# Wider conversion blocks (384 or 512 columns instead of 256) for the later weights of an attention and mixer kernel

## The chip, the cores and the metric

The kernel runs on one core of a Trainium2 chip. The metric is the device time of one execution in microseconds (us), from start to end. Before the change it was 773.08 us, the median of three runs (770.61, 773.08, 774.40).

## What is computed

The reference has three parts in a row, for 4 batches of 576 tokens with 512 features:

```python
# 1. attention, 8 heads of 64: a local band plus an average-pooled attention
out = repeat(softmax(qd kd^T) vd, 4) + softmax(band(q k^T)) v
# 2. mixer: a token mix and a channel mix, both with ReLU
u = x + (relu(x^T w_tok1) w_tok2)^T
x = u + relu(u w_ch1) w_ch2                # w_ch1 512x1536, w_ch2 1536x512
# 3. a second mixer
theta = x w_theta                          # 512x512
y = w_tok_r (x cos theta) + w_tok_i (x sin theta)
u = x + y
out = u + relu(u w_ch)                     # 512x512
```

The attention inputs are float32. The weights arrive as 64-bit floats, since they were divided by a square root on the host. The kernel reads them as pairs of 32-bit words and turns each into two float32 parts, a high and a low one, whose sum carries more digits than one of them. All large products are made from such parts: a matmul of high with high, one of high with low, one of low with high.

## The kernel before

**Order of the work.** The attention, the token mix and the first half of the channel mix for batches 0 and 1 are interleaved by a list written out by hand (`ORDER`). After it come the loops of line 644 (first half of the hidden channels, batches 2 and 3), of line 677 (second half, batches 0 to 3) and of line 780 (the second mixer). TensorE is never told to wait for a stage as a whole: the framework's scheduler lays out one instruction order for each engine from the program's order, from the dependencies and from an estimate of each instruction's length, and on the chip each engine takes its list in order.

**The channel mix** (`channel_mix`, line 187) works on one batch and, by `th`, on one half of its tokens (288) at a time. It loads `ut` through the SyncE queue (L198), splits it into `uh` and `ul` (L97 on ScalarE, L98 on VectorE), and makes six blocks of hidden channels, each of 12 matmuls (L101 to L103). Each block leaves PSUM by two instructions, a ReLU on ScalarE (L217) and a subtraction on VectorE (L218), both at high priority. These give `g`, the high and low part of the hidden values. Then come four blocks of outputs, each of 18 matmuls (L226, L227 with the high `g` of all six hidden blocks, then L229 with the low `g`), and each is added to `ut` by VectorE (L231). One such half of a batch has 144 matmuls, 72 of each product.

**The conversion** (`weights`, line 109) takes one block of a weight: a DMA into a staging buffer `raw` (L114, here through ScalarE's queue, `rawq[0] = nc.scalar`), then

- ScalarE: L122 (low word to `wf`) and L124 (absolute value of the high word to `ww`),
- GpSimd: L125, a clamp of `ww`,
- VectorE: L129, L137 and L140 on the bits of `ww`, L147 on `wf`,
- ScalarE: L148, the high part; GpSimd: L149, a subtraction; and L150, an addition that gives the low part, in turn on GpSimd and on VectorE.

The staging buffers `ww`, `we` and `wf` have 3 slots each, and `raw` has 4. `load_split` (line 155) makes a list of such steps for one weight, column block by column block and in each over the row blocks of 128.

**What is converted beside the channel mix.** The second half of `w_ch1` (tiles `c11h`, `c11l`: 12 blocks of 256 columns), the second half of `w_ch2` (`c21h`, `c21l`: 12 blocks), `w_theta` (`thh`, `thl`: 8 blocks), the joined `w_tok_r` and `w_tok_i` (`wrh`, `wrl`: 18 blocks of 288) and `w_ch` (`wch`, `wcl`: 8 blocks), 58 blocks in this order. `channel_mix` takes them from `aside`, 6 at the end of each half of a batch: in four halves by line 645, in six by line 678. `c11` and `c21` are needed by the loop of line 677, the others by that of line 780.

Of the kernel before, what the change touches and what calls it, by code (L numbers as in the profile page):

```python
# [36 lines left out]
B, H, S, D = 4, 8, 576, 64  # L37
DM = H * D
# [23 lines left out]
def kernel(  # L62
# [19 lines left out]
    nc = tc.nc  # L82
# [5 lines left out]
    xT_d = [dram.tile([DM, S], F32, name=f"xT_{b}") for b in range(B)]  # L88
# [15 lines left out]


    clamps = chain(islice(cycle([pool] * 4 + [dve]), 33), repeat(pool))
    rawq = [nc.sync]

    def weights(stage, hi, lo, parts, adder=dve):

        n = hi.shape[-1]
        raw = stage.tile([128, n], parts[0][2].dtype, tag="raw", name="raw", bufs=4)
        for p0, p1, src in parts:
            rawq[0].dma_start(raw[p0:p1], src)  # L114
        if raw.dtype == I64:
            words = raw.bitcast(U32).rearrange("p (n t) -> p n t", t=2)
            high = raw.bitcast(F32).rearrange("p (n t) -> p n t", t=2)[:, :, 1]
            w = stage.tile([128, n], F32, tag="ww", name="ww")
            e = stage.tile([128, n], BF16, tag="we", name="we")
            f = stage.tile([128, n], BF16, tag="wf", name="wf")  # L120

            act.activation(f, words[:, :, 0], AF.Copy, scale=2.0**-52)  # L122

            act.activation(w, high, AF.Abs)  # L124
            next(clamps).tensor_scalar(  # L125
                out=w, in0=w, scalar1=F64_LEAST, scalar2=F64_MOST, op0=ALU.max, op1=ALU.min
            )
            wu = w.bitcast(U32)
            dve.tensor_scalar(  # L129
                out=wu,  # L130
                in0=wu,
                scalar1=3,
                scalar2=0x3FFFFFF8,
                op0=ALU.logical_shift_left,
                op1=ALU.bitwise_and,
            )
            dve.scalar_tensor_tensor(  # L137
                out=wu, in0=words[:, :, 1], scalar=0xC0000000, in1=wu, op0=ALU.bitwise_and, op1=ALU.bitwise_or
            )
            dve.tensor_scalar(  # L140
                out=e.bitcast(U16),
                in0=w.bitcast(U16).rearrange("p (n t) -> p n t", t=2)[:, :, 1],
                scalar1=0xFF80,
                scalar2=None,
                op0=ALU.bitwise_and,
            )
            dve.tensor_tensor(out=f, in0=f, in1=e, op=ALU.mult)  # L147
            act.copy(hi, w)  # L148
            pool.tensor_tensor(out=w, in0=w, in1=hi.bitcast(F32), op=ALU.subtract)  # L149
            adder.tensor_tensor(out=lo, in0=w, in1=f, op=ALU.add)  # L150
        else:
            adder.tensor_copy(hi, raw)
            pool.tensor_tensor(out=lo, in0=raw, in1=hi.bitcast(F32), op=ALU.subtract)

    def load_split(pool_, stage, name, src, nk, n, chunk, adders=(pool, dve)):

        hi = pool_.tile([128, nk, n], F32R, name=name + "h")
        lo = pool_.tile([128, nk, n], F32R, name=name + "l")
        steps = []
        for c in range(0, n, chunk):  # L160
            for k in range(nk):
                def step(k=k, c=slice(c, c + chunk), adder=adders[len(steps) % len(adders)]):
                    weights(stage, hi[:, k, c], lo[:, k, c], [(0, 128, src[k * 128 : (k + 1) * 128, c])], adder)
                steps.append(step)
        return hi, lo, steps
# [7 lines left out]
    NCH = DCH // 2  # L173
    NCB = NCH // 128

    def channel_weights(pool_, stage, half):
        c = slice(half * NCH, (half + 1) * NCH)
        adders = (pool, dve) if half else (pool,)
        h1, l1, s1 = load_split(pool_, stage, f"c1{half}", w_ch1[:, c], 4, NCH, 256, adders)
        h2, l2, s2 = load_split(pool_, stage, f"c2{half}", w_ch2[c, :], NCB, DM, 256, adders)  # L180
        return (h1, l1, h2, l2), s1 + s2


# [3 lines left out]
    def channel_mix(b, half, src, dst, w, mmb, queue, aside=(), per=0):  # L187

        w1h, w1l, w2h, w2l = w
        for th in range(2):  # L190
            t = slice(th * HALF, (th + 1) * HALF)
            at = f"{b}_{half}_{th}"
            here = half == 0 and b in DIRECT
            if here:
                ut = mixed[b][th]
            else:
                ut = b2.tile([128, 4, HALF], F32, tag="ut", name=f"ut_{at}")
                queue.dma_start(ut, uT_d[b][:, t].rearrange("(k p) n -> p k n", p=128))  # L198
            uh = b1.tile([128, 4, HALF], F32R, tag="uh", name=f"uh_{at}")
            ul = b1.tile([128, 4, HALF], F32R, tag="ul", name=f"ul_{at}")  # L200
            if here:
                for kb in range(4):
                    split(uh[:, kb, :], ul[:, kb, :], ut[:, kb, :])
            else:
                split(uh, ul, ut)
            if half:
                queue.dma_start(ut, src[:, t].rearrange("(k p) n -> p k n", p=128))
            hs = []
            for cb in range(NCB):
                c = slice(cb * 128, (cb + 1) * 128)  # L210
                ps = mmb.tile([128, 512], F32, tag="mb", name=f"c1_{at}_{cb}")
                for kb in range(4):
                    mm3(ps[:, 0:HALF], w1h[:, kb, c], w1l[:, kb, c], uh[:, kb, :], ul[:, kb, :], kb == 0, kb == 3)
                h1 = hp.tile([128, HALF], F32R, tag="h1", name=f"g1_{at}_{cb}")
                h2 = hp.tile([128, HALF], F32R, tag="h2", name=f"g2_{at}_{cb}")
                with tc.high_priority(offset=2000):
                    act.activation(h1, ps[:, 0:HALF], AF.Relu)  # L217
                    dve.scalar_tensor_tensor(  # L218
                        out=h2, in0=ps[:, 0:HALF], scalar=0.0, in1=h1.bitcast(F32), op0=ALU.max, op1=ALU.subtract
                    )  # L220
                hs.append((h1, h2))
            for db in range(4):
                d = slice(db * 128, (db + 1) * 128)
                ps = mmb.tile([128, 512], F32, tag="mb", name=f"c2_{at}_{db}")
                for cb in range(NCB):
                    pe.matmul(ps[:, 0:HALF], w2h[:, cb, d], hs[cb][0], start=(cb == 0), stop=False)  # L226
                    pe.matmul(ps[:, 0:HALF], w2l[:, cb, d], hs[cb][0], start=False, stop=False)  # L227
                for cb in range(NCB):
                    pe.matmul(ps[:, 0:HALF], w2h[:, cb, d], hs[cb][1], start=False, stop=(cb == NCB - 1))  # L229
                with tc.high_priority(offset=2000):  # L230
                    dve.tensor_tensor(out=ut[:, db, :], in0=ps[:, 0:HALF], in1=ut[:, db, :], op=ALU.add)  # L231
            queue.dma_start(dst[:, t].rearrange("(k p) n -> p k n", p=128), ut)
            for st in islice(aside, per):
                st()

    with ExitStack() as actx:
        sb1 = actx.enter_context(tc.tile_pool(name="a1", bufs=1))
        sb2 = actx.enter_context(tc.tile_pool(name="a2", bufs=2))
        stg = actx.enter_context(tc.tile_pool(name="stg", bufs=3))
# [53 lines left out]
        low, lowsteps = channel_weights(wlow, stg, 0)  # L293
# [329 lines left out]
        for e in ORDER:  # L623
            if e == "S":
                spare.release()
                spare = None
                mmb = tc.alloc_tile_pool(name="mmb", bufs=2, space=PSUM, side="right")
# [7 lines left out]
            else:  # L635
                event(e[0], int(e[1:]))

    rawq[0] = nc.scalar
    mmw = tc.alloc_tile_pool(name="mmw", bufs=6, space=PSUM)
    wide = tc.alloc_tile_pool(name="whigh", bufs=1)  # L640
    stg = tc.alloc_tile_pool(name="stg", bufs=3)
    high, highsteps = channel_weights(wide, stg, 1)
    aside = iter(highsteps)
    for b in range(sum(e[0] == "C" for e in ORDER), B):
        channel_mix(b, 0, None, xT_d[b], low, mmb if b == B - 2 else mmw, nc.sync, aside, 6)
    wlow.release()
    cw = ctx.enter_context(tc.tile_pool(name="cw", bufs=1, side="right"))
    thh, thl, thsteps = load_split(cw, stg, "th", w_theta, 4, DM, 256)
    wch, wcl, wcsteps = load_split(cw, stg, "wc", w_ch, 4, DM, 256)
    wrh, wrl, wrsteps = load_split(cw, stg, "wr", w_ri, 9, S, HALF)  # L650
    aside = iter(thsteps + wrsteps + wcsteps)
    cx = ctx.enter_context(tc.tile_pool(name="cx", bufs=2, side="right"))
# [22 lines left out]
        return xh, xl  # L675

    for b in range(B):
        channel_mix(b, 1, xT_d[b], xT_d[b], high, mmw, nc.sync, aside, 6)
        if b == B - 2:
            xx = stage_x(0, mmw)  # L680
            stg.release()
            cs = ctx.enter_context(tc.tile_pool(name="cs", bufs=1, side="right"))
            xhl = split_x(0, xx[0])
# [183 lines left out]
```

## Time and profile before

| what | value |
|---|---|
| median of three runs | 773.08 us |
| profiled execution | 770.8 us, of which its span on the engines is 768.9 us |
| TensorE matmul | 714.6 us busy (93%), 7872 matmuls |
| VectorE | 509.6 us (66%) |
| ScalarE | 333.6 us (43%) |
| GpSimd | 265.4 us (35%) |
| mean granted TensorE clock | 0.973 of full speed |

A busy TensorE is not TensorE at its peak, since matmuls overlap. The shares are means over stages that differ: the conversions of the last 58 blocks lie between about 314 and 480 us of the span, and what they cost is read there.

### The profile page before, as it was taken

The page shows a single profiled execution, that of the slowest core. Times are in us where ns is not written, and L with a number is a line of the kernel's source. Part 1 is how long each engine was busy: PE and PEld are TensorE (multiplying, and loading weights), DVE is VectorE, ACT ScalarE, POOL GpSimd, SP SyncE. Part 2 cuts the span into 40 slices and gives each one's busy share as a digit, 9 for nine tenths or more (in the row PEclk, how much of TensorE's full clock was granted, in tenths as well). Part 3 has the DMA queues.
Part 4 walks back from the last instruction along what each step waited for, and adds up shares of the span by engine and source line. Part 5 has one row for each costly group of instructions (what it writes and reads, how often), then busy time and mean ns, then how long its engine had stood idle before and what let it go on. Part 6 is the DMA issues. An engine that isn't in the chain of part 4 may idle for free.

```text
span 768.9 us, 19289 instructions
## 1 busy us (share of the span) xinstructions
PE 714.6 (93%) x7872; PEld 672.6 (87%) x7872; DVE 509.6 (66%) x1151; ACT 333.6 (43%) x774; POOL 265.4 (35%) x292
## 2 busy tenths in 40 slices
PE   8586978789999999899999899999999999999998
PEld 5365766679979999899999889999999999999998
DVE  5998999985565334499999999422585365554432
ACT  1564656534244222356555555231574254353310
POOL 1767687671021000398998887000000000000000
PEclk9777999899999999999999999999999999999999
DMA  9578656654343220545565856330000400300101
GB/s 274 179 200 220 185 147 196 180 167 141 129 134 102 66 78 32 165 153 170 171 186 172 256 166 192 116 93 32 32 1 1 131 1 1 124 1 1 64 1 62
DMA packets 61897, 90.73 MB, mean 118 GB/s; under 512 B 10096, under 2 KB 39920, under 8 KB 61808
## 3 DMA queue, kind: packets, MB, share of 16 engines
q1 hardware_dynamic: 53456, 73.70, 31.5%
q10 hardware_dynamic: 8352, 15.80, 6.7%
q8 instruction: 62, 1.02, 0.6%
q14 instruction: 27, 0.22, 0.1%
HBM read 69.42 MB, written 20.05 MB: 116 GB/s over the span
## 4 chain that ended last, share of the span: by engine, by line
PE 60%; DVE 23%; DMA 6%; issue 6%; POOL 2%; SPq 2%; ACT 1%; ACTq 0%; DVEq 0%; POOLq 0%
PE y L103 5%; PE y L101 5%; PE y L102 5%; PE c L229 4%; PE c L226 4%; PE c L227 4%; DVE ww L137 4%; DVE ww L129 3%; PE c L101 3%; PE c L103 3%; PE c L102 3%; DVE wf L147 3%; DVE we L140 3%; PE th L101 2%; PE th L102 2%
## 5 line engine op out<-in xcount | busy, mean ns | idle before, releaser
L125 POOL TENSOR_SCALAR ww<-ww 128x256 f32<-128x256 f32 (+1 forms) x85 | 100.3, 1182 | 55.6 <-ACT ww L124 51.2
L103 PE MATMUL y<-wrh,zl 128*128 128x288 f32 x256 | 75.7, 296 | 0.0
L102 PE MATMUL y<-wrl,zh 128*128 128x288 f32 x256 | 75.6, 295 | 0.0
L101 PE MATMUL y<-wrh,zh 128*128 128x288 f32 x256 | 75.6, 296 | 0.0
L218 DVE SCALAR_TENSOR_TENSOR g<-c,g 128x288 fp32r<-128x288 f32 x96 | 43.2, 451 | 44.0 <-ACT g L217 43.9
L217 ACT ACTIVATE g<-c 128x288 fp32r<-128x288 f32 x96 | 38.9, 408 | 57.0 <-PE c L103 55.2
L101 PE MATMUL c<-uh,c10h 128*128 128x288 f32 x192 | 58.6, 310 | 3.7 <-DVE g L218 3.7
L122 ACT ACTIVATE wf<-raw 128x256 bf16<-128x256 uint32 (+1 forms) x91 | 40.4, 444 | 45.5 <-DVE wrl L150 8.3
L226 PE MATMUL c<-g,c21h 128*128 128x288 f32 x192 | 54.6, 306 | 5.7 <-ACT g L217 5.7
L102 PE MATMUL c<-ul,c10h 128*128 128x288 f32 x192 | 57.2, 299 | 1.0 <-DVE ul L98 1.0
L103 PE MATMUL c<-uh,c10l 128*128 128x288 f32 x192 | 57.5, 300 | 0.0
L101 PE MATMUL c<-uh,c11h 128*128 128x288 f32 x192 | 56.9, 296 | 0.0
L102 PE MATMUL c<-ul,c11h 128*128 128x288 f32 x192 | 56.6, 295 | 0.0
L103 PE MATMUL c<-uh,c11l 128*128 128x288 f32 x192 | 56.5, 294 | 0.0
L129 DVE TENSOR_SCALAR ww<-ww 128x256 uint32<-128x256 uint32 (+1 forms) x91 | 50.0, 551 | 6.3 <-POOL ww L125 5.8
L227 PE MATMUL c<-g,c21l 128*128 128x288 f32 x192 | 53.7, 301 | 0.0
L226 PE MATMUL c<-g,c20h 128*128 128x288 f32 x192 | 53.0, 302 | 0.7 <-ACT g L217 0.5
L227 PE MATMUL c<-g,c20l 128*128 128x288 f32 x192 | 53.3, 300 | 0.0
L137 DVE SCALAR_TENSOR_TENSOR ww<-raw,ww 128x256 uint32<-128x256 uint32 (+1 forms) x91 | 49.1, 541 | 1.5
L102 PEld LDWEIGHTS y<-wrl,zh 128*128 128x128 f32 x256 | 48.1, 188 | 0.0
L101 PEld LDWEIGHTS y<-wrh,zh 128*128 128x128 f32 x256 | 48.1, 188 | 0.0
L103 PEld LDWEIGHTS y<-wrh,zl 128*128 128x128 f32 x256 | 48.1, 188 | 0.0
(201 smaller groups left out, 2243.5 us busy)
## 6 DMA issues: line engine op xcount, KB each, us to landing
raw<-w_ch ACTq DMA_DIRECT2D x32, 256.0 KB, 2.8
ut<-uT SPq DMA_DIRECT2D x14, 576.0 KB, 4.5
xT<-ut SPq DMA_DIRECT2D x14, 576.0 KB, 3.2
raw<-w_ch SPq DMA_DIRECT2D x24, 256.0 KB, 3.5
vd<-vtok SPq DMA_DIRECT2D x8, 650.0 KB, 7.2
raw<-w_ri ACTq DMA_DIRECT2D x18, 288.0 KB, 3.1
k<-kT SPq DMA_DIRECT2D x16, 291.0 KB, 5.7
q<-qT SPq DMA_DIRECT2D x16, 288.0 KB, 4.8
```

What stands on the lines that cost most here:

```text
L101: pe.matmul(out, lh, rh, start=start, stop=False)
L102: pe.matmul(out, lh, rl, start=False, stop=False)
L103: pe.matmul(out, ll, rh, start=False, stop=stop)
L122: act.activation(f, words[:, :, 0], AF.Copy, scale=2.0**-52)
L125: next(clamps).tensor_scalar(out=w, in0=w, scalar1=F64_LEAST, scalar2=F64_MOST, op0=ALU.max, op1=ALU.min)
L129: dve.tensor_scalar(out=wu, in0=wu, scalar1=3, scalar2=0x3FFFFFF8, op0=ALU.logical_shift_left, op1=ALU.bitwise_and,)
L137: dve.scalar_tensor_tensor(out=wu, in0=words[:, :, 1], scalar=0xC0000000, in1=wu, op0=ALU.bitwise_and, op1=ALU.bitwise_or)
L217: act.activation(h1, ps[:, 0:HALF], AF.Relu)
L218: dve.scalar_tensor_tensor(out=h2, in0=ps[:, 0:HALF], scalar=0.0, in1=h1.bitcast(F32), op0=ALU.max, op1=ALU.subtract)
L226: pe.matmul(ps[:, 0:HALF], w2h[:, cb, d], hs[cb][0], start=(cb == 0), stop=False)
L227: pe.matmul(ps[:, 0:HALF], w2l[:, cb, d], hs[cb][0], start=False, stop=False)
L229: pe.matmul(ps[:, 0:HALF], w2h[:, cb, d], hs[cb][1], start=False, stop=(cb == NCB - 1))
```

## The change

The later weights are converted in wider blocks: `c11` in blocks of 384 columns, `c21`, `th` and `wc` in blocks of 512. The joined token weights `wr` keep 288. The `raw` staging buffer has 3 slots instead of 4 in these stages, and `channel_mix` takes 4 steps (line 645) or 5 (line 678) at the end of a half instead of 6. In blocks: `c11` 12 to 8, `c21` 12 to 6, `th` 8 to 4, `wc` 8 to 4, `wr` 18 as before, so 58 become 40.

```diff
-    rawq = [nc.sync]
+    rawq, rawn = [nc.sync], [4]
...
-        raw = stage.tile([128, n], parts[0][2].dtype, tag="raw", name="raw", bufs=4)
+        raw = stage.tile([128, n], parts[0][2].dtype, tag="raw", name="raw", bufs=rawn[0])
...
-        h1, l1, s1 = load_split(pool_, stage, f"c1{half}", w_ch1[:, c], 4, NCH, 256, adders)
-        h2, l2, s2 = load_split(pool_, stage, f"c2{half}", w_ch2[c, :], NCB, DM, 256, adders)
+        n1, n2 = (NCH // 2, DM) if half else (256, 256)
+        h1, l1, s1 = load_split(pool_, stage, f"c1{half}", w_ch1[:, c], 4, NCH, n1, adders)
+        h2, l2, s2 = load_split(pool_, stage, f"c2{half}", w_ch2[c, :], NCB, DM, n2, adders)
...
-    rawq[0] = nc.scalar
+    rawq[0], rawn[0] = nc.scalar, 3
...
-        channel_mix(b, 0, None, xT_d[b], low, mmb if b == B - 2 else mmw, nc.sync, aside, 6)
+        channel_mix(b, 0, None, xT_d[b], low, mmb if b == B - 2 else mmw, nc.sync, aside, 4)
...
-    thh, thl, thsteps = load_split(cw, stg, "th", w_theta, 4, DM, 256)
-    wch, wcl, wcsteps = load_split(cw, stg, "wc", w_ch, 4, DM, 256)
+    thh, thl, thsteps = load_split(cw, stg, "th", w_theta, 4, DM, DM)
+    wch, wcl, wcsteps = load_split(cw, stg, "wc", w_ch, 4, DM, DM)
...
-        channel_mix(b, 1, xT_d[b], xT_d[b], high, mmw, nc.sync, aside, 6)
+        channel_mix(b, 1, xT_d[b], xT_d[b], high, mmw, nc.sync, aside, 5)
```

## Rows read from the trace of the kernel before

**Rows 1.** Stretches: length, then busy PE, PEld, DVE, ACT, POOL (instructions), clock, DMA, GB/s.

```profile
373.00:405.00 32.00, 31.07 (x230) 30.41 (x229) 30.61 (x74) 19.14 (x48) 29.26 (x32) 1.00 0.65 198
405.00:460.00 55.00, 50.19 (x354) 48.45 (x353) 52.49 (x110) 30.53 (x73) 46.29 (x46) 0.97 0.63 195
460.00:481.47 21.47, 20.55 (x151) 19.84 (x150) 20.28 (x48) 11.87 (x29) 16.06 (x18) 1.00 0.66 207
481.47:500.65 19.18, 19.18 (x146) 19.18 (x145) 8.46 (x16) 4.75 (x9) 0.00 (x0) 1.00 0.32 99
```

**Rows 2.** Timeline of PE (start, length, what): the starts of products.

```profile
362.70 0.29 PE L226 MATMUL c<-g,c20h 128*128 128x288 f32 x1
...
374.05 0.30 PE L101 MATMUL c<-uh,c11h 128*128 128x288 f32 x1
...
383.65 0.30 PE L226 MATMUL c<-g,c21h 128*128 128x288 f32 x1
...
481.47 0.29 PE L101 MATMUL c<-uh,c11h 128*128 128x288 f32 x1
...
491.07 0.30 PE L226 MATMUL c<-g,c21h 128*128 128x288 f32 x1
...
500.65 0.60 PE L665 MATMUL ct<-idt,cx 128*128 128x128 f32 x4
```

**Rows 3.** Who waited for whom, 310 to 485 us: total us, times, longest us.

```profile
ACT c21h L148 <- DVE ww L137: 6.8, 9, 2.0
PE c L226 <- ACT g L217: 6.2, 10, 1.6
```

**Rows 4.** Timelines of POOL, DVE and ACT around 361 us and around 428 us.

```profile
360.32 1.24 POOL L125 TENSOR_SCALAR ww<-ww 128x256 f32<-128x256 f32 x1 [0.29 <-ACT ww L124]
361.25 0.29 DVE L147 TENSOR_TENSOR wf<-wf,we 128x256 bf16<-128x256 bf16 x1
...
426.94 0.87 POOL L149 TENSOR_TENSOR ww<-ww,wrh 128x288 f32<-128x288 f32 x1
427.06 0.92 DVE L129 TENSOR_SCALAR ww<-ww 128x288 uint32<-128x288 uint32 x1
...
428.75 0.43 ACT L148 CAST wrh<-ww 128x288 fp32r<-128x288 f32 x1 [0.93 <-DVE ww L137]
429.14 0.41 ACT L217 ACTIVATE g<-c 128x288 fp32r<-128x288 f32 x1
```

**Rows 5.** Two stretches of 2 us, in the columns of rows 1.

```profile
430.00:432.00 2.00, 2.00 (x10) 2.00 (x9) 1.97 (x6) 2.00 (x5) 1.71 (x3) 0.50 1.05 391
432.00:434.00 2.00, 2.00 (x12) 2.00 (x12) 1.97 (x4) 1.03 (x3) 1.69 (x3) 0.69 0.93 303
```

**Rows 6.** Groups by shape, 310 to 485 us: busy us, mean ns, idle before.

```profile
L150 DVE TENSOR_TENSOR thl<-ww,wf 128x256 fp32r<-128x256 f32 x4 | 1.7, 413 | 0.0
L150 DVE TENSOR_TENSOR wrl<-ww,wf 128x288 fp32r<-128x288 f32 x9 | 4.0, 445 | 0.0
```

**Rows 7.** Timeline of DVE: two additions and what follows the first.

```profile
384.48 0.41 DVE L150 TENSOR_TENSOR c21l<-ww,wf 128x256 fp32r<-128x256 f32 x1
384.81 0.28 DVE L147 TENSOR_TENSOR wf<-wf,we 128x256 bf16<-128x256 bf16 x1
...
479.56 0.43 DVE L150 TENSOR_TENSOR wcl<-ww,wf 128x256 fp32r<-128x256 f32 x1 [0.26 <-POOL ww L149]
```

**Rows 8.** Timelines of ACT and PE where the conversions begin.

```profile
314.18 1.38 ACTq L114 DMA_DIRECT2D raw<-w_ch  x3
320.51 0.43 ACT L122 ACTIVATE wf<-raw 128x256 bf16<-128x256 uint32 x1 [1.53 <-DMA raw<-w_ch]
...
322.10 0.40 PE L101 MATMUL c<-uh,c10h 128*128 128x288 f32 x1 [1.66 <-DVE g L218]
```

**Rows 9.** DMA issues, 310 to 485 us: count, KB each, median us to landing.

```profile
raw<-w_ch ACTq DMA_DIRECT2D x32, 256.0 KB, 2.8
raw<-w_ri ACTq DMA_DIRECT2D x18, 288.0 KB, 3.1
```

## Prediction

> **What bounds the kernel now.** I read the table of stretches first. While the conversions run, TensorE is busy nearly all the time, but VectorE is as full: 30.61 of 32 us, 52.49 of 55, 20.28 of 21.47 [rows 1]. In the stretch after them TensorE has no gap and VectorE is under half busy. Next I read the starts of the products in TensorE's timeline, because a modelled busy time hides small gaps. Undisturbed, one half of a batch takes 500.65 - 481.47 = 19.18 us, its second product 500.65 - 491.07 = 9.58 [rows 2]. The five halves before took 481.47 - 374.05 = 107.4 us [rows 2], so 11.5 us more than 5 x 19.18, some 2.3 each. The loss sits in the second product: that of 362.70 lasted to 374.05, 11.35 us in place of 9.58, so 1.77 lost [rows 2]. The list of waits says why: L226 stood ten times for the ReLU L217, 6.2 us, and ScalarE's L148 nine times for VectorE's L137 in one weight alone, 6.8 us [rows 3]. The timelines join the two. GpSimd's subtraction L149 ran from 426.94 to 427.81; VectorE's L129, begun at 427.06, ended just after it, 0.92 us long; L137 followed, L148 on ScalarE waited for it, and the ReLU behind L148 began only at 429.14 [rows 4], with TensorE waiting. In this gap the granted clock fell to 0.50 for 430 to 432 us, the lower of its two levels, 1.2 GHz [rows 5], after TensorE had stood; 10 and 12 matmuls in 2 us each there, where the pace of rows 2 gives 15. So the ceiling of any gain is the loss of this stage, some 15 us (11.5 + 1.8, and 1.7 at the start, below); from 481 us on TensorE alone sets the time.
>
> **The change part by part.** *Fewer, longer instructions.* 40 blocks of 256 become 22 wider ones: 18 are gone, the columns stay. On VectorE L150 takes 413 ns for 256 columns and 445 for 288 [rows 6]: 1.0 ns a column, so 413 - 256 = 157 ns of a block are not owed to its columns. A block has four more VectorE instructions, and every second block an L150; I give each the same 157 ns as an estimate: 4.5 x 0.157 = 0.71 us for a block gone. That is the upper end. The lower one: L147 starts 0.33 us after an L150 of 0.41 us [rows 7], so 0.08 of the 157 ns lies beside the next instruction: 4.5 x 0.077 = 0.35 us. Between them 0.53, so VectorE is rid of 18 x 0.53 = 9.5 us (6.3 to 12.8). It is the fullest engine, so the last block, which ended at 479.99 [rows 7], would end at about 470.5. ScalarE saves too, but it has 30.53 of 55 us busy [rows 1]: nothing, beside other work. If its cover goes, it is again the wait for L137 that shows, priced below.
>
> *What this does for TensorE.* The last disturbed half (460.62 to 481.47; its length is near the mean of the five) lost 1.7 us, and in its second product, from 470.2 on. With the conversions over by then this goes: **-1.7 us** (0 to -1.7). For the second products from 362.70 and 383.65, with `c21` and `th` beside them, two things can happen. If as many columns per half are converted as now (8 blocks a half, so 4 mergers), VectorE has 4 x 0.53 = 2.1 us less to do in a half that loses 1.77, and the loss goes: -3.4 for both. If the columns come faster instead, VectorE is as full as before and the loss stays: 0. And if each wait is as long as its instruction, it doubles: +3.4. Nothing in the order holds the columns back, as VectorE at 30.61 of 32 shows, so I take a value near the middle one: **-0.8 us**.
>
> *The waits on the shared memory path.* A VectorE instruction of the conversion that starts beside GpSimd's two-input L149 ends after it, while one beside the clamp L125 does not wait for its end: L147 took 0.29 us at 361.25, inside a clamp that ran until 361.56 [rows 4]. Half as many waits of twice the length change VectorE's sum by nothing, which is what I take; their length is priced in the second rival. The Trainium skill, "SBUF — State Buffer", section "SBUF: two separate sides", states that VectorE and GpSimd share a port pair under an exclusive lock, and that whichever starts first holds it for its whole instruction while the other fully blocks. The trace agrees for L149 and not for the clamp. By that rule the wider clamp would stop VectorE for all of its length, and my sum would come to no gain (third rival).
>
> *The start.* Three loads are issued from 314.18 on; ScalarE stood 1.53 us for the third until 320.51, and TensorE then 1.66 us [rows 8]. The first blocks are 384 KB instead of 256. 288 KB landed in 3.1 us and 256 in 2.8 [rows 9]: 0.3 us for 32 KB, so +1.2 for 128. The far end: all 320.51 - 314.18 = 6.33 us scale by 1.5, +3.2; the near end 0, if the ReLU stands ahead of that wait in ScalarE's list. The scheduler can place it so; I take **+0.5 us**.
>
> *Slots and steps.* With 3 `raw` slots two loads run ahead of the block in work. Blocks come every 163 / 58 = 2.8 us now, some 4 after, so a load has 8 us for the 3 to 5 it takes: nothing; if this cover is gone, ScalarE waits for a load as in [rows 8], 1.5 us each. Steps of 4 and 5 for 6 only set the place in the program, and blocks don't keep to it: the last of `c21`, put behind the half that ends at 374.05, ran until 384.89 [rows 2, 7], and the last of `wc`, put behind the one that ends at 500.65, by 479.99. Nothing. The loads issued from ScalarE's queue fall by 18; ScalarE has room. The `wr` blocks are the same; their losses, with the clock's fall, may move either way by what the fall cost, 5 + 3 matmuls of 0.13 us [rows 5], 1.1 us.
>
> *Sum.* -1.7 - 0.8 + 0.5 = -2.0 us. The profiled execution was 770.8 us (span 768.9 and 1.9 around it), so 768.8 against it. The median of the runs, 773.08, stands 2.3 above that execution: 771.1 us.
>
> **The rivals.**
> 1. *VectorE drops below TensorE's pace.* The 2.1 us less per half are more than the loss of 1.77, so the small difference decides. -1.7 - 3.4 = -5.1, with the clock's fall gone -6.2: 768.0 to 766.9. For it: the loss is a thin excess of VectorE's work. Against it: the full VectorE of rows 1, which takes all that is offered. Chance 0.33.
> 2. *Longer waits, slower.* A ReLU behind an L148 waits for an L137 that waits for a GpSimd instruction of 512 columns. Place: the second products from 362.70 and 383.65 and that beside `wc`. If each loss doubles: 1.77 + 1.7 + 1.7 and the start's 0.5 make +5.7: 778.8. It decides once a wait for L137 (longest 2.0 us [rows 3]) grows past what six PSUM buffers and the first matmuls cover. For it: rows 4. Against it: half as many waits. Chance 0.15.
> 3. *GpSimd is the bound.* It is busy 29.26 of 32 us [rows 1]; if its clamp held VectorE off, the conversion could not go faster. Then only the start counts: 773.6. That is where the page's rule on the lock would lead; the clamp in rows 4 speaks against it. Chance 0.05.
> 4. *The weights come late.* `c21` is cut into full rows, so the first output block needs all six, by 383.65 + 10 x 0.13 = 385.0; now the last was needed only from the third output block on, about 388.4, and was done at 384.89 [rows 2, 7]. If nothing is saved and the start costs its 3.2, TensorE stands until 388.1: +3.1, so 776.2. Ten blocks less make 5.3 us of room. Chance 0.05.
>
> **How the numbers follow.** A measurement of this kernel can tell about 0.5% (3.9 us) from no change: 769.2 and 776.9 are the borders. The forecast (0.42) lies between them, with 0.03 of it below and 0.03 above, for the `wr` halves and the start; rivals 3 and 4 (0.10) between them too; rival 1 (0.33) below; rival 2 (0.15) above, with its smaller prices inside. So faster 0.35, same 0.47, slower 0.18, the last with the tails of the forecast. The range takes in rival 1 with the clock's 1.1 us and one more lost half of the `wr` blocks (some 1.8), and most of the way to rival 2: 765.0 to 777.5. The forecast's own is 768.5 to 774.5.
>
> **What would show it.** Right: 22 wide blocks; the wide VectorE additions L150 near 0.67 us (413 + 256 ns); the last `wcl` by about 470 us; a half of 19.2 us from then on; TensorE's waits for L217 in the stage of the same number or fewer; the start's gap 1.7 to 2.5 us. If the last `wcl` comes at 475 or later, the saving on VectorE was misjudged. If it comes at 470 and the time rises all the same, the longer waits decided: L226's wait for L217 would pass 9 us. If the halves with `c21` and `th` shrink to 19.2 us, rival 1 holds. The step most likely to be wrong is the -0.8, a choice between ends of both signs.

## The result, and the profile after

The changed kernel takes 780.91 us (median of 7 runs, 776.97 to 783.28) against 771.11 us (7 runs, 770.16 to 774.40): ratio 1.0119, 95% interval 1.0090 to 1.0148. It is slower, by more than the range of the prediction allowed. The profiled execution is 780.9 us with a span of 779.1, so 10.1 us longer than that of before. In its lines the ReLU is L220, the first product of outputs L229, and in the conversion the clamp is L126, the bit operations L130, L138 and L141, the multiplication L148, the high part L149, the subtraction L150, the addition L151.

The stretches, in the columns of [rows 1], the first three those of [rows 1], the fourth the half in which most was lost, and two of 2 us within it:

```profile
373.00:405.00 32.00, 30.54 (x225) 29.76 (x224) 30.90 (x48) 14.50 (x29) 27.85 (x20) 1.00 0.52 157
405.00:460.00 55.00, 49.31 (x347) 46.18 (x345) 52.67 (x107) 31.45 (x74) 45.15 (x44) 1.00 0.70 221
460.00:481.47 21.47, 19.27 (x141) 18.80 (x141) 15.31 (x24) 5.47 (x12) 11.08 (x7) 1.00 0.38 118
466.38:491.25 24.87, 20.95 (x147) 20.72 (x146) 15.35 (x27) 6.71 (x13) 4.70 (x4) 0.93 0.43 136
482.00:484.00 2.00, 0.33 (x2) 0.33 (x3) 2.00 (x4) 2.00 (x6) 0.00 (x0) 1.00 0.48 176
486.00:488.00 2.00, 2.00 (x10) 2.00 (x10) 1.05 (x3) 0.00 (x0) 0.00 (x0) 0.50 0.24 29
```

VectorE is as full as before until 460 us, with fewer instructions (48 for 74 in the first row). In the third row it is not full any more, 15.31 of 21.47, where before it was at 20.28. So the conversions do end sooner. Yet TensorE has fewer matmuls there than before, 141 for 151.

TensorE's timeline gives the lengths of the halves, as in [rows 2]:

```profile
314.16 0.29 PE L101 MATMUL c<-uh,c10h 128*128 128x288 f32 x1
...
322.85 0.40 PE L101 MATMUL c<-uh,c10h 128*128 128x288 f32 x1 [0.54 <-DVE g L221]
...
346.50 0.40 PE L229 MATMUL c<-g,c20h 128*128 128x288 f32 x1 [1.22 <-ACT g L220]
...
348.71 0.40 PE L229 MATMUL c<-g,c20h 128*128 128x288 f32 x1 [0.35 <-ACT g L220]
...
377.36 0.30 PE L101 MATMUL c<-uh,c11h 128*128 128x288 f32 x1
...
466.38 0.29 PE L101 MATMUL c<-uh,c11h 128*128 128x288 f32 x1
...
483.67 0.40 PE L229 MATMUL c<-g,c21h 128*128 128x288 f32 x1 [3.92 <-ACT g L220]
...
491.25 0.29 PE L101 MATMUL c<-uh,c11h 128*128 128x288 f32 x1
```

The halves, each from the start of its first product to the start of the next, stand in the first two columns of the table; the other two are experiments (`e1_split_behind` and `e6_paced`), below. "Beside" says what most of the conversion works on in the kernel before.

| beside | before | after | split behind | paced, 256 |
|---|---|---|---|---|
| `c21` | 20.87 (from 353.18) | 21.64 (from 355.72) | 21.62 | |
| `c21`, `th` | 20.84 | 21.53 | 21.55 | 19.18 (from 375.91) |
| `th`, `wr` | 21.02 | 23.34 | 25.73 | 19.18 |
| `wr` | 23.27 | 23.10 | 20.03 | 19.18 |
| `wr` | 21.44 | 21.05 | 22.59 | 19.42 |
| `wc` | 20.85 (to 481.47) | 24.87 (to 491.25) | 19.17 | 19.18 (to 472.05) |

Before the first of these halves TensorE is 355.72 - 353.18 = 2.5 us late. Most of that was there before a wide block was: the product at 314.16 stands at 311.85 in the kernel before,

```profile
311.85 0.29 PE L101 MATMUL c<-uh,c10h 128*128 128x288 f32 x1
```

so TensorE was 2.3 us late when the first wide block was loaded (316.49). In the experiments below, with wide blocks or without, this product starts anywhere from 312.14 to 315.38; these 2.3 us are not shown to be the change's. From it to the first of these halves it is 41.56 us for 41.33, only 0.2 more, although the two waits above, 1.22 + 0.35, are in it. The next five halves are 110.66 us for 107.44, 3.2 more. The last is 24.87 for 20.85, 4.0 more. Together that is 9.7 of the 10.1. The last is the half from which the prediction took 1.7 us off.

Who waited for whom, 310 to 485 us, as in [rows 3]:

```profile
PE c L229 <- ACT g L220: 11.9, 13, 3.9
...
ACT wch L149 <- DVE ww L138: 7.8, 3, 4.7
ACT cxh L97 <- DMA cx<-xT: 6.7, 1, 6.7
...
ACT c21h L149 <- DVE ww L138: 5.1, 6, 2.2
```

TensorE's wait for the ReLU has gone from 6.2 to 11.9 us. The waits for `c21h` are fewer and no shorter (6 for 9, longest 2.2 for 2.0). One row was not in the list of before at all: a copy of L97 that waits 6.7 us for a load. The timeline of ScalarE, with the loads on SyncE's queue and the last VectorE addition of the conversion, shows where it stands:

```profile
472.13 0.62 ACT L149 CAST wch<-ww 128x512 fp32r<-128x512 f32 x1 [4.72 <-DVE ww L138]
472.65 1.30 ACT L220 ACTIVATE g<-c 128x288 fp32r<-128x288 f32 x4
...
474.44 0.69 DVE L151 TENSOR_TENSOR wcl<-ww,wf 128x512 fp32r<-128x512 f32 x1 [0.82 <-POOL ww L150]
...
476.43 0.50 SPq L663 DMA_DIRECT2D cx<-xT  x1
476.98 0.50 SPq L659 DMA_DIRECT2D cx<-xT  x1
...
480.71 2.60 ACT L97 CAST cxh<-cx 128x640 fp32r<-128x640 f32 x4 [6.75 <-DMA cx<-xT]
483.22 0.70 ACT L220 ACTIVATE g<-c 128x288 fp32r<-128x288 f32 x2
```

The last `wcl` is done at 475.1. With the conversion out of the way, the next thing in ScalarE's list is the split of `cx` for the second mixer (`split_x`, called in the loop of line 677), ahead of the last two ReLUs of the half. Its load was issued only at 476.43 and 476.98, so ScalarE stood for 6.75 us, copied for 2.60 us, and only then made the two ReLUs at 483.22. TensorE stood 3.92 us; for 482 to 484 us it has 0.33 of 2 us busy. Then its clock was granted at 0.50, the lower of its two levels, for 486 to 488 us, with 10 matmuls there, as in [rows 5]. In the kernel before, the same copies stand behind the last `wch`, their load was issued ten us ahead of them, and the ReLU after them, which belongs to the next half, is held by nothing but TensorE:

```profile
469.69 0.50 SPq L660 DMA_DIRECT2D cx<-xT  x1
...
477.18 0.41 ACT L148 CAST wch<-ww 128x256 fp32r<-128x256 f32 x1 [1.18 <-DVE ww L137]
480.02 2.61 ACT L97 CAST cxh<-cx 128x640 fp32r<-128x640 f32 x4 [2.44 <-DVE wcl L150]
483.26 0.41 ACT L217 ACTIVATE g<-c 128x288 fp32r<-128x288 f32 x1 [0.63 <-PE c L103]
```

So the load has hardly moved: it was issued 9.1 us after the start of this half and is issued 10.1 us after it now. What moved is the end of the conversion, from 19.4 us after that start to 8.7, and the copies with it.

Last, the groups of VectorE and GpSimd by shape, in the columns of [rows 6], the first line from the kernel before:

```profile
L129 DVE TENSOR_SCALAR ww<-ww 128x256 uint32<-128x256 uint32 x40 | 22.1, 553 | 1.0 <-POOL ww L125 0.9
...
L130 DVE TENSOR_SCALAR ww<-ww 128x512 uint32<-128x512 uint32 x14 | 15.9, 1135 | 1.0 <-POOL ww L126 1.0
L138 DVE SCALAR_TENSOR_TENSOR ww<-raw,ww 128x512 uint32<-128x512 uint32 x14 | 12.9, 919 | 0.2
L148 DVE TENSOR_TENSOR wf<-wf,we 128x512 bf16<-128x512 bf16 x14 | 8.6, 615 | 0.4
...
L151 DVE TENSOR_TENSOR thl<-ww,wf 128x512 fp32r<-128x512 f32 x2 | 1.4, 677 | 0.0
...
L150 POOL TENSOR_TENSOR ww<-ww,c21h 128x512 f32<-128x512 f32 x6 | 9.1, 1519 | 0.0
```

The undisturbed addition of 512 columns, 677 ns, is what the prediction gave it (0.67). L130 is not: with 256 columns its group of before has a mean of 553 ns, and twice that is 1106, so a merger of two saves nothing on it. GpSimd's subtraction has grown from 880 ns (256 columns, `c21h`, before) to 1519.

### The profile page after: what moved, and what is told of

Same layout as the page of the kernel before. It is cut to its first block, busy times and chain, and to the rows that moved or that the text cites. A ratio compares the mean times of both kernels' runs of the same rounds, so it can differ in the third digit from the quotient of the medians.

```text
span 779.1 us, 19006 instructions
## 1 busy us (share of the span) xinstructions
PE 718.1 (92%) x7872; PEld 674.6 (87%) x7872; DVE 505.7 (65%) x1070; ACT 324.5 (42%) x720; POOL 255.3 (33%) x247
## 4 chain that ended last, share of the span: by engine, by line
PE 57%; DVE 23%; DMA 9%; issue 5%; POOL 2%; ACT 2%; SPq 0%; DVEq 0%; ACTq 0%; POOLq 0%
PE y L101 5%; PE y L103 5%; PE y L102 5%; DVE ww L138 4%; PE c L232 4%; PE c L230 3%; PE c L229 3%; DMA q<-qT 3%; PE c L101 3%; DVE ww L130 3%; PE c L102 3%; PE c L103 3%; DVE wf L148 3%; DVE we L141 2%; PE th L101 2%
## 5 line engine op out<-in xcount | busy, mean ns | idle before, releaser
L126 POOL TENSOR_SCALAR ww<-ww 128x256 f32<-128x256 f32 (+3 forms) x67 | 97.2, 1452 | 61.0 <-ACT ww L125 58.6
L221 DVE SCALAR_TENSOR_TENSOR g<-c,g 128x288 fp32r<-128x288 f32 x96 | 42.9, 451 | 46.6 <-ACT g L220 46.2
L220 ACT ACTIVATE g<-c 128x288 fp32r<-128x288 f32 x96 | 37.8, 406 | 65.5 <-PE c L103 63.8
L229 PE MATMUL c<-g,c21h 128*128 128x288 f32 x192 | 54.3, 305 | 10.1 <-ACT g L220 9.6
L229 PE MATMUL c<-g,c20h 128*128 128x288 f32 x192 | 54.2, 307 | 2.5 <-ACT g L220 2.3
L123 ACT ACTIVATE wf<-raw 128x256 bf16<-128x256 uint32 (+3 forms) x73 | 36.8, 504 | 41.0 <-DVE c21l L151 5.6
L138 DVE SCALAR_TENSOR_TENSOR ww<-raw,ww 128x256 uint32<-128x256 uint32 (+3 forms) x73 | 49.7, 683 | 0.9
L130 DVE TENSOR_SCALAR ww<-ww 128x256 uint32<-128x256 uint32 (+3 forms) x73 | 47.2, 647 | 3.5 <-POOL ww L126 3.2
L234 DVE TENSOR_TENSOR ut<-c,ut 128x288 f32<-128x288 f32 x56 | 25.2, 451 | 36.5 <-PE c L232 36.4
```

The source lines that it names most:

```text
L126: next(clamps).tensor_scalar(out=w, in0=w, scalar1=F64_LEAST, scalar2=F64_MOST, op0=ALU.max, op1=ALU.min)
L130: dve.tensor_scalar(out=wu, in0=wu, scalar1=3, scalar2=0x3FFFFFF8, op0=ALU.logical_shift_left, op1=ALU.bitwise_and,)
L138: dve.scalar_tensor_tensor(out=wu, in0=words[:, :, 1], scalar=0xC0000000, in1=wu, op0=ALU.bitwise_and, op1=ALU.bitwise_or)
L221: dve.scalar_tensor_tensor(out=h2, in0=ps[:, 0:HALF], scalar=0.0, in1=h1.bitcast(F32), op0=ALU.max, op1=ALU.subtract)
```

## The experiments

Three theories, which may hold together. **A, the order at the end:** the copies of `cx`, waiting for their load, stand ahead of two ReLUs; this is worth the last half, some 5.7 us (24.87 - 19.17). **B, longer waits:** a VectorE instruction beside a GpSimd instruction of 512 columns ends late, L149 behind it too, and the ReLU behind that; this is the second rival. **C, the slots:** with 3 `raw` buffers loads come late. All kernels do the whole of the computation. Ratios are to the kernel before, timed beside each.

**Theory A: the copies two ReLUs later.** `e1_split_behind` is the changed kernel with the copies put behind the ReLU that is seventh from the end of those traced so far.

```diff
-                    act.activation(h1, ps[:, 0:HALF], AF.Relu)
+                    relus.append(act.activation(h1, ps[:, 0:HALF], AF.Relu))
...
-            xhl = split_x(0, xx[0])
+            with tc.issue_after(relus[-7].ins):
+                xhl = split_x(0, xx[0])
```

> The wide blocks kept; only the four copies that split cx stand two ReLUs later in ScalarE's list, behind the last ReLU of the half that they delayed. Theory A (the conversions end earlier, the scheduler puts these copies ahead of two ReLUs, and their load comes late): the half from 466.4 to 491.3 us, 24.9 us long, falls to 19.5 to 20.9, TensorE's wait of 3.9 us goes, the time is 4 to 5.5 us less than that of the changed kernel, some 1.005 of the kernel before. Theory B (all of the loss is longer waits behind longer instructions): the half stays at 24 to 25 us and the time at 1.012.

Measured: 774.81 us, ratio 1.0021 (0.9998 to 1.0044). ScalarE's timeline (here the ReLU is L221), then the half as a stretch:

```profile
471.86 0.62 ACT L149 CAST wch<-ww 128x512 fp32r<-128x512 f32 x1 [4.73 <-DVE ww L138]
472.39 1.31 ACT L221 ACTIVATE g<-c 128x288 fp32r<-128x288 f32 x4
474.41 0.41 ACT L221 ACTIVATE g<-c 128x288 fp32r<-128x288 f32 x1 [0.71 <-PE c L103]
476.01 0.41 ACT L221 ACTIVATE g<-c 128x288 fp32r<-128x288 f32 x1 [1.19 <-PE c L103]
...
480.98 2.60 ACT L97 CAST cxh<-cx 128x640 fp32r<-128x640 f32 x4
```

```profile
466.16:485.33 19.17, 19.17 (x146) 19.17 (x145) 13.96 (x25) 6.95 (x13) 4.66 (x4) 1.00 0.53 165
```

The two ReLUs come at 474.41 and 476.01, waiting for TensorE alone, and the half takes 19.17 us, undisturbed. The copies themselves begin at 480.98, 0.27 us later than in the changed kernel, so nothing was lost by it. The medians differ by 6.1 us (the ratios by 0.0098, 7.6 us), the half by 5.7. Theory A holds for this part. With it the change is about even with before, not ahead of it: the 1.7 us that the last half gave back are used up elsewhere.

**Where is the rest?** `e2_c_wide` widens `c11` and `c21` alone (3 slots, steps of 4, then 6); `e3_th_wc_wide` widens `th` and `wc` alone (3 slots, steps of 6, then 5).

```diff
# e2_c_wide, against the changed kernel
-    thh, thl, thsteps = load_split(cw, stg, "th", w_theta, 4, DM, DM)
-    wch, wcl, wcsteps = load_split(cw, stg, "wc", w_ch, 4, DM, DM)
+    thh, thl, thsteps = load_split(cw, stg, "th", w_theta, 4, DM, 256)
+    wch, wcl, wcsteps = load_split(cw, stg, "wc", w_ch, 4, DM, 256)
# e3_th_wc_wide, against the changed kernel
-        n1, n2 = (NCH // 2, DM) if half else (256, 256)
+        n1, n2 = 256, 256
```

> Only c11 and c21 in wide blocks (384, 512), th and wc at 256 with 6 steps, three raw slots. If the loss of each half goes with the blocks converted beside it: the half with c11 and the two with c21 lose what they do in the changed kernel (1.8 and 1.4 us more than before), the later ones what they did before, and the cx copies come as before; 3 us more than the kernel before, 1.004. If what counts is only the late accident of the cx copies: the same as before, within 1 us.

> Only th and wc in blocks of 512, c11 and c21 at 256 with 6 steps, three raw slots. If the loss goes with the blocks beside it: the halves until 395 us as before, those with th and wr after it 2 us longer, and the cx copies late as in the changed kernel, 4 us: 6 us more than before, 1.008. If the wide c11 and c21 did the harm: as before.

Measured: 774.02 us, 1.0010 (0.9989 to 1.0031) for `c`, and 779.81 us, 1.0094 (1.0057 to 1.0130) for `th` and `wc`. Nearly all of the loss is with `th` and `wc`. For `c` the ratio is that of its second forecast, and the first, 1.004, lies just outside the interval, although the profiled halves beside `c21` are longer, 21.82 us twice for 20.87 and 20.84. For `th` and `wc` the time came as forecast, but not the places: the copies were not late, and the half from 375.68, where the first `th` blocks begin, was already 24.03 us for 20.84. There the last disturbed half is long too, 25.00 us, but not for the copies: its `wch` waits, with a ReLU behind it, and TensorE behind that (the timeline; ReLU L220, between the two at 482.11):

```profile
481.59 0.62 ACT L149 CAST wch<-ww 128x512 fp32r<-128x512 f32 x1 [3.79 <-DVE ww L138]
...
482.57 0.40 PE L229 MATMUL c<-g,c21h 128*128 128x288 f32 x1 [2.37 <-ACT g L220]
```

This is theory B's chain. Here the last conversion ended at 486.4 us, so the wait fell in that half and not before it.

**Theory B: GpSimd's two-input instructions in halves.** `e5_pool_halves` is the changed kernel with L150, and L151 where GpSimd makes it, as two instructions of half the columns, if a block has 384 columns or more. `e8_halves_behind` is the same with the edit of `e1_split_behind`.

```diff
-            pool.tensor_tensor(out=w, in0=w, in1=hi.bitcast(F32), op=ALU.subtract)
-            adder.tensor_tensor(out=lo, in0=w, in1=f, op=ALU.add)
+            m = n if n < 384 else n // 2
+            for a in range(0, n, m):
+                s = slice(a, a + m)
+                pool.tensor_tensor(out=w[:, s], in0=w[:, s], in1=hi[:, s].bitcast(F32), op=ALU.subtract)
+            for a in range(0, n, m if adder is pool else n):
+                s = slice(a, a + (m if adder is pool else n))
+                adder.tensor_tensor(out=lo[:, s], in0=w[:, s], in1=f[:, s], op=ALU.add)
```

> The changed kernel with GpSimd's two-input instructions (subtraction and addition) on 384 or 512 columns cut into two halves each, all else wide. Theory L (the extra loss is VectorE held for a whole long GpSimd instruction): TensorE's waits for the ReLU and for the subtraction in the halves with c11, c21 and th fall back, 3 us less than the changed kernel. Rival (the length of VectorE's and ScalarE's own instructions, or the order): no change, or a little more for the added instructions' fixed part.

> The changed kernel with GpSimd's two-input instructions in halves and the cx copies behind the ReLUs of their half. If the two edits act on the same loss (the cx copies' place), the sum is no better than either alone: 773 to 775, 1.001. If the halves cured something else (locks in the halves with c11, c21 and th), their gains add: 768 to 770, 0.996.

Measured: 773.58 us, 1.0014 (0.9990 to 1.0039), and 773.71 us, 1.0025 (1.0004 to 1.0045). Halving takes the loss away, but it doesn't show why: the conversion then ends at 477.7 us for 475.1, and the copies of `cx` wait only 2.1 us for their load. That removes most of theory A's accident as well, which is why the two edits together gain nothing more than either alone. The halves beside `wr` moved both ways (23.31, 21.61, 23.85 and 24.80, 21.00, 23.94 us). As to theory B this pair is inconclusive.

**Theory C: the slots alone.** `e4_three_slots` is the kernel before with 3 `raw` slots in these stages.

```diff
-        raw = stage.tile([128, n], parts[0][2].dtype, tag="raw", name="raw", bufs=4)
+        raw = stage.tile([128, n], parts[0][2].dtype, tag="raw", name="raw", bufs=rawn[0])
...
-    rawq[0] = nc.scalar
+    rawq[0], rawn[0] = nc.scalar, 3
```

> The kernel before with one edit of the change alone: three raw slots instead of four, blocks of 256 and 6 steps as they were. Theory (a load has time enough with two ahead): the same as before within 2 us, ScalarE's waits for raw loads in the stage as before (2.7 us). Rival (the third slot's loss makes loads late and carries part of the change's loss): 3 us or more over before, and more wait for raw.

Measured: 774.85 us, 1.0034 (1.0017 to 1.0052): some 2.6 us, where the prediction had nothing. ScalarE's waits for loads, 312 to 492 us:

```profile
ACT wf L122 <- DMA raw<-w_ch: 5.2, 9, 1.1
...
ACT wf L122 <- DMA raw<-w_ri: 3.3, 4, 1.5
...
ACT wf L122 <- DMA raw<-w_theta: 0.8, 1, 0.8
```

This lies between its two forecasts, the waits nearer to the second. They make 9.3 us; before, the list had 2.7 and 0.5. In the changed kernel they are 0.5 (`w_ch`) and 2.1 (`w_ri`), 2.6 us, so with wide blocks three slots cost ScalarE no more than four did with narrow ones. The changed kernel with four slots was not tried, so how much of its loss belongs to them stays open.

**Theory B again, without VectorE's excess.** In all these kernels the conversion takes whatever VectorE has left, so a longer wait and a fuller engine can't be told apart. `e6_paced` (the kernel before) and `e7_wide_paced` (the changed kernel) put each half's steps, in the loop of line 677, behind the last ReLU of that half in ScalarE's list, the loads issued there too. So 6 blocks, or 5, are converted beside a half, and no more.

```diff
-            for st in islice(aside, per):
-                st()
+            with tc.issue_after(relus[-1].ins) if half else ExitStack():
+                for st in islice(aside, per):
+                    st()
```

> The kernel before, blocks of 256 and four slots; in the second half of the channels each group of six steps is put behind the last ReLU of the half of a batch after which it is listed, so that the blocks of th, wr and wc cannot run ahead (8 a half now). Theory (the losses of these halves come from a VectorE that is offered more than 19.2 us of work in a half): with 6 blocks VectorE has some 18.3 us, the halves from 395 us on fall from 20.9 to 23.3 us to about 19.5 to 20.5, 4 to 7 us less than before in all, 0.993. Rival (the losses come from where a ReLU happens to stand in ScalarE's list, whatever the density): the same as before within 2 us.

> The changed kernel with the same pacing (five steps a half behind the last ReLU of that half). The conversions then end about when they do not meet the cx copies early: the 3.9 us wait goes, as with the copies moved, and the wr halves shorten as in the paced kernel before; the halves with wide c11 and c21 stay as in the changed kernel. 768 to 772, 0.996. If long instructions do harm wherever they meet the end of a first product, th (four of 512 in one group) and wc keep a loss of 2 us each and it is no faster than before.

Measured: `e6_paced` 762.95 us, 0.9874 (0.9849 to 0.9900), faster than both kernels of this case; `e7_wide_paced` 773.05 us, 1.0007 (0.9985 to 1.0028). The same stretch of each, `e6_paced` first:

```profile
395.00:416.00 21.00, 21.00 (x159) 21.00 (x159) 18.97 (x44) 11.23 (x29) 15.87 (x18) 1.00 0.60 185
```

```profile
395.00:416.00 21.00, 18.13 (x123) 17.67 (x122) 17.08 (x25) 9.10 (x20) 15.43 (x11) 0.92 0.43 127
```

The gain of `e6_paced`, 9.7 us, is more than its theory's 4 to 7. The edit does two things at once, fewer blocks beside a half and a fixed place for them in ScalarE's list, and no run separates these. With 256 columns and pacing TensorE has no gap, and VectorE is 18.97 of 21 us busy. With 512 columns VectorE has less to do, 17.08, and still TensorE has 123 matmuls for 159: the half from 395.28 takes 24.12 us. So here the sum of VectorE's work is not what counts; the length of the pieces is the candidate. The timeline of `e7_wide_paced` (GpSimd, VectorE and ScalarE; ReLU L221) shows one such wait:

```profile
396.72 1.92 POOL L126 TENSOR_SCALAR ww<-ww 128x512 f32<-128x512 f32 x1
...
397.87 0.68 DVE L138 SCALAR_TENSOR_TENSOR ww<-raw,ww 128x512 uint32<-128x512 uint32 x1
...
400.34 1.33 POOL L150 TENSOR_TENSOR ww<-ww,thh 128x512 f32<-128x512 f32 x1 [0.43 <-DVE we L141]
400.45 1.50 DVE L148 TENSOR_TENSOR wf<-wf,we 128x512 bf16<-128x512 bf16 x1
401.63 1.35 POOL L151 TENSOR_TENSOR thl<-ww,wf 128x512 fp32r<-128x512 f32 x1
401.87 1.65 DVE L138 SCALAR_TENSOR_TENSOR ww<-raw,ww 128x512 uint32<-128x512 uint32 x1
403.56 0.62 ACT L149 CAST thh<-ww 128x512 fp32r<-128x512 f32 x1 [4.04 <-DVE ww L138]
404.08 0.41 ACT L221 ACTIVATE g<-c 128x288 fp32r<-128x288 f32 x1
```

L138 takes 0.68 us at 397.87, beside the clamp. At 401.87, beside GpSimd's addition, it takes 1.65, and L148 before it 1.50, beside the subtraction. L149 has waited 4.04 us, and the ReLU comes behind it. The rest of this trace agrees. Of its fourteen L138 of 512 columns, four began beside a two-input GpSimd instruction, the one shown among them; each ended 0.54 or 0.55 us after that instruction's end and took 1.11 to 1.68 us. Five ran inside a clamp and took 0.67 to 0.98, the others 0.68 or 0.69. In `e6_paced` the L148 of `thh` with 256 columns waits 1.8 us at most in this stretch.

**The same in parts.** `e10_paced_halves` is `e7_wide_paced` with GpSimd's instructions in halves, as in `e5_pool_halves`. `e11_c_wide_paced` and `e12_th_wc_paced` are `e2_c_wide` and `e3_th_wc_wide` with the pacing; their edits are those shown, together.

> The wide kernel paced, with GpSimd's subtraction and addition in halves of at most 256 columns. In the paced wide kernel VectorE is not full (17.1 of 21 us from 395 us on) and three of its instructions in a row took 1.35 to 1.65 us, each beside one GpSimd instruction of 1.3 us, before the ReLU behind them could start. Theory L (VectorE is held for a whole two-input GpSimd instruction, so its length sets the wait): with halves of 0.74 us the 24 us halves fall to about 21 and the time by 4 to 6 us, to 768. Rival (the chain of wide instructions on every engine sets the wait, whoever holds whom, and VectorE meets the second half as well): within 2 us of the paced wide kernel, 773.

> Paced, only c11 and c21 in wide blocks (before the paced part), th and wc at 256, three raw slots. If wide c11 and c21 cost little (1 us) and three slots little once the blocks are paced: 763 to 766, 0.990. If the three slots delay the paced blocks too (loads late at the start of each group): 768 or more.

> Paced, only th and wc in blocks of 512, c11 and c21 at 256, three raw slots. If the loss of the paced wide kernel over the paced kernel before (10 us) lies with th and wc: 770 to 773, with halves of 22 to 24 us where th and wc are converted and 19.2 where wr is. If it lies with c11 and c21 or their order: 765 or less.

Measured:

| kernel | us | ratio, 95% | halves from about 376 us |
|---|---|---|---|
| `e6_paced`, all 256 | 762.95 | 0.9874 (0.9849 to 0.9900) | 19.18, 19.18, 19.18, 19.42, 19.18 |
| `e11_c_wide_paced` | 764.79 | 0.9896 (0.9854 to 0.9938) | 19.19, 19.18, 19.18, 19.18, 19.18 |
| `e10_paced_halves` | 767.33 | 0.9917 (0.9886 to 0.9947) | 19.18, 20.98, 23.22, 19.18, 19.18 |
| `e12_th_wc_paced` | 771.21 | 0.9984 (0.9965 to 1.0003) | 19.18, 22.10, 22.75, 19.20, 19.17 |
| `e7_wide_paced` | 773.05 | 1.0007 (0.9985 to 1.0028) | 19.18, 24.12, 19.98, 21.30, 19.18 |

Now the parts separate. Wide `c` blocks, converted ahead of these halves, change little (+1.8 us over `e6_paced`, with intervals that overlap). Wide `th` and `wc` cost 8.3 us, with the second and third half long, where `th` is converted and `wr` follows; the half after the five, where `wc` ends, is 24.66 us for the 22.29 of `e6_paced`, with waits of `wch` of 2.4 to 3.6 us. These two kernels have 3 slots and `e6_paced` 4; since `e11_c_wide_paced` has 3 and five undisturbed halves, the slots alone do not make the difference. Splitting GpSimd's two-input instructions alone gives back 773.05 - 767.33 = 5.7 us, with the half from 395 us at 20.98 for 24.12. The stretch of `e10_paced_halves` has more work and fewer gaps than that of `e7_wide_paced`:

```profile
395.00:416.00 21.00, 19.42 (x147) 19.19 (x145) 18.84 (x34) 9.24 (x20) 19.71 (x19) 1.00 0.56 167
```

VectorE is busier (18.84 for 17.08 us) and TensorE loses less (147 matmuls for 123). From 375 to 502 us TensorE's wait for the ReLU falls from 6.6 us (longest 2.4) to 3.6 (longest 1.6), and the longest wait of `thh` from 4.0 to 2.9. Theory L's forecast came true for the time and for that half, and its rival's (773) did not. So that VectorE is held is shown, and that this makes the loss with wide blocks is well supported; how much of the time it makes is less sure. The next half grew, from 19.98 to 23.22, some 2 us of the gain lie before these halves, beside `c11` and `c21`, and the six times fall into two groups (762.25 and 763.00; 767.14 to 767.97). More instructions can also change the scheduler's order, which no run holds fixed. And in the changed kernel itself, without pacing, theory B stays argued.

## Why the prediction was wrong

The saving on VectorE came about. What failed is the step that turned it into time for TensorE.

**What bounds the kernel: right.** VectorE takes all that is offered, and TensorE loses some 2 us a half by it. `e6_paced` bears the reading out: without the excess the halves from 375.91 to 472.05 take 96.1 us, where before the five to 481.47 took 107.4, and the kernel gains some 9.7 us (772.39 x 0.0126, the median beside it and its ratio).

**VectorE's saving: the low end.** The 22 wide blocks take 75.3 us of VectorE for the 83.2 of the 40 narrow ones (sums of the groups by shape), so 7.9 us, inside 6.3 to 12.8. The `wr` blocks took 1.2 us more. The last `wcl` is 4.9 us earlier, at 475.1, not 9.5, and the prediction set 475 as the mark from which this term counts as misjudged. But the mark was a clock time, and the first loads were 2.3 us later (316.49 for 314.18): from first load to last `wcl` it is 158.6 us for 165.8, 7.2 less. The term is at the low end because it priced an instruction by undisturbed additions; L130 gave only 0.5 us of the 7.9 (21.6 for 22.1), and VectorE's additions took 0.5 more than before (10.0 for 9.5).

**"The last disturbed half ... With the conversions over by then this goes: -1.7": the step that failed.** The conversions were over, as it says, and the half grew by 4.0 us. The prediction did not ask what is late next on ScalarE once the conversion is gone: the copies of `cx`, ahead of two ReLUs. ScalarE stood for them from 473.96 on, and their load was issued only at 476.43. `e1_split_behind` moves them and the half takes 19.17 us, the -1.7 that was forecast (20.85 - 19.17). This step turned from -1.7 to +4.0, 5.7 us of the error.

**"I take a value near the middle one: -0.8": on the other side.** The first two halves of the table took 43.17 us for 41.71, +1.5, between the middle end 0 and the far end +3.4. TensorE's wait for the ReLU in them is 2.2 us for 0.9, which is most of it. That is the second rival's direction, but these halves don't show its cause: VectorE is as full as before there (41.78 of 43.17 us, before 40.10 of 41.71), and the waits for `c21h` are hardly longer. The rival's mark, a wait of L229 for the ReLU over 9 us, was passed with 11.9, but only by the 3.9 that are the copies' doing; without them it is 8.0. The three after them, beside `wr` for most of their length and left at nothing with 1.1 us either way, took 67.49 for 65.73, +1.8; single ones can't be compared, as `e1_split_behind` shows with 25.73, 20.03 and 22.59.

**"Half as many waits of twice the length change VectorE's sum by nothing": beside the point.** With the work paced, VectorE's sum fell and TensorE still lost (`e7_wide_paced`): to the ReLU the longest wait ahead of it matters more. The rows for it were there, [rows 4], and stood as a rival with 0.15.

**The start, +0.5: near the size, not by its path.** From the product at 314.16 (311.85 before) to the first half of the table it took 0.2 us more. TensorE's gap is 0.54 us for 1.66 [rows 8], the wrong sign for the load's wait that was priced. Behind it, from 322.85, it takes 32.87 us where it took 31.08; the two waits for ReLUs, 1.57 us, are most of that. That the two nearly cancel is luck, and no experiment separates them.

**Slots and steps: nothing.** With 256 columns three slots cost 2.6 us (`e4_three_slots`), against the prediction's argument of 8 us of cover; with wide blocks ScalarE's waits for loads did not grow. That blocks don't keep to their place in the program held; `e6_paced` shows what it is worth if they are made to.

**The shared path: right.** A wide clamp does not hold VectorE off to its end: in `e7_wide_paced` L138 ran 0.68 us inside a clamp of 1.92, while beside L150 and L151 VectorE's instructions end after them. So the third rival, GpSimd as the bound, did not come. The rule of the Trainium skill, "SBUF — State Buffer", section "SBUF: two separate sides", that whichever engine starts first holds the shared ports for its whole instruction, agrees with the trace for two-input GpSimd instructions and not for the clamp. The section says this, of VectorE's side, only for instructions with two inputs in SBUF (against a GpSimd instruction that reads SBUF) or in a two-port mode, a condition that the prediction left out; L138 has two such inputs and the clamp reads SBUF, so the disagreement stands. **The weights** were not late either: the list of TensorE's waits has none for `c21`.

**The chances.** By the prediction's own working they add up to 0.36 for faster and 0.46 for same, where it wrote 0.35 and 0.47; nothing hangs on it.

## What to carry to other kernels

When a change takes work off an in-order queue, look up what stands next in that queue and whether its inputs are there by then: what moves up can stop more than what went away. Where a latency-critical instruction shares a queue with background work, look at the longest single wait ahead of it and not only at the sum: merging background instructions can cost time though it saves work. And if background work fills an engine to the brim, give it out at the pace of the work in front: that gave 1.3% here, and widening gave nothing on top.

## What was not expected of the hardware

VectorE instructions in a row were each held by a two-input GpSimd instruction: L148 for 1.50 us, where its mean with 512 columns in the changed kernel is 0.62, and L138 for 1.65, where it took 0.68 beside the clamp. TensorE's wait of 3.92 us was followed by a granted clock of 0.50 for 486 to 488 us, though it was busy again from 483.67 on; so a long wait was paid for twice, as the short one at 428 us in the kernel before [rows 5]. And three buffers in place of four cost 2.6 us although a block came only every 2.8 us and its load took about as long.
